# The issue points of indirect row transfers, set by a running count of streamed matmul time

## The chip, the cores and the metric

The kernel runs on one core of a Trainium2 chip. The metric is device time in microseconds (us), the median of three runs. TensorE (PE in the profile) does the matrix products, VectorE (DVE), ScalarE (ACT) and GpSimd (POOL) the elementwise work, SyncE (SP) only issues transfers. Transfers whose rows are scattered by a list of indices ("indirect") are issued by POOL.

## The reference

Two stages follow each other. A long convolution of each of 8 sequences (5056 steps, 128 channels, f32) with one filter, by FFT:

```
Xf = np.fft.rfft(x, n=L, axis=1); Hf = np.fft.rfft(h, n=L, axis=0)     # L = 2 * 5056
y = np.fft.irfft(Xf * Hf[None, :, :], n=L, axis=1)[:, :S, :]
```

Then each of the 40448 resulting rows goes through one of 16 experts, picked by two argmaxes (4 groups, 4 experts in each), and is scaled by the two softmax weights:

```
h = np.maximum(xg[mask_e] @ w1[g, e], 0.0)       # 128 -> 1024
out[tok_idx] = combined[:, None] * (h @ w2[g, e])  # 1024 -> 128
```

## The kernel before

The FFT is a chain of small matmuls in three rounds (`ROUNDS`), of three sequences each; the filter takes one place in round 0. In a round, `stage1` transforms along one axis, `groups` transforms along the other, multiplies by the filter's spectrum and transforms back (`forward`, `product`, `inverse`), and `side` does the last transform, one octave (8 of 64 steps) at a time. `side` of a round runs beside stage 1 and groups of the next round, and that of round 2 beside the experts. An octave gives 10 or 15 tiles of 128 token rows; it computes their gate, and with it the place of each row in a table `srt` in DRAM, sorted by expert. Each tile is then scattered into `srt` by one indirect transfer (`scatter`, line 873; 320 of them). From step 0 of the experts on, blocks of 512 rows of one expert are gathered from `srt` (`ffn_x`, line 1284), multiplied through both layers as split f32r matmuls (`mm1`, lines 1383 to 1385, `mm2`, lines 1401 to 1403; 8 steps for a block), transposed and scaled into a tile `orow` (`out_store`), and scattered into `out` by indirect transfers of 128 rows (`scatter_out`, line 1450). Blocks 2 to 29 send half their rows into a buffer `outd` first, and fetch them back later (`take`), so that these go out with later blocks. 59 blocks are fixed at build; the rest of each expert runs in a tail of conditional blocks (`ffn_tail`).

The order on each engine is that in which the program records its work, and a table `main` of closures sets it, into which `weave` sets the steps of `side`. Rows that wait for their scatter stand in the list `self.sends`, output rows in `self.due`. In the kernel before, transfers are sent at fixed places of the program: one `send` in each `product`, after an `inverse`, after every fourth step of stage 1, after pieces of `side` (`beside`), and one after most expert steps; `scatter_out` at certain steps of a block's plan ("o"). Each transfer that is sent so is made to wait for a matmul by `behind`, by way of `self.mark`, the matmul recorded last at certain lines:

```
    def behind(self, ins):
        if self.mark is not None:
            info = mybir.DependencyInfo(mybir.DependencyClass.Sync, mybir.DependencyReason.DATA)
            self.tc.add_manual_dep(ins.ins, self.mark.ins.name, info, reason="transfers are issued one by one")
```

POOL works in order. So a transfer goes out when its matmul has ended, its data are there, and POOL has issued the one before it. `drain` empties `self.sends` before the expert blocks that read the rows of a round. What waits for a transfer's landing: the reuse of `rw` tiles (ACT, line 798), of `orow` tiles (DVE, line 1421), the gathers from `srt` (SP, line 1284), the fetching back (`take`, SP, line 1444), and the eighth transfer after it on POOL (eight semaphores, DMASW0 to DMASW7, take turns).

## Time and profile before

| | us |
|---|---|
| median of 3 runs | 1722.85 (1707.83, 1722.85, 1723.93) |
| profiled execution | 1721.78 |
| its span, first to last instruction | 1720.1 |
| PE busy in the span | 1627.1 (95%) |
| DVE, ACT, POOL busy | 1311.6, 1084.3, 753.7 |
| mean granted clock of TensorE | 0.987 of full speed |

The rounds' stage 1 and groups fill the span up to about 650 us, round 0 without any indirect transfer; the first stands at 190.5 us. The experts' fixed blocks run from about 656 to 1450 us, the tail from there to the end. A PE that is busy 95% of the time leaves some 93 us in which it waits, and where these lie is what the rows below are for.

### The profile page before, as it was taken

To read this page: it belongs to the slowest core of one execution; us is meant where nothing else is said; L and a number is where in the kernel's file an instruction comes from. 1 tells how busy PE (TensorE), PEld (TensorE's weight loads), DVE (VectorE), ACT (ScalarE), POOL (GpSimd) and SP (SyncE) were. 2 spreads that over 40 slices of the span, in tenths; PEclk is the share of its full clock that TensorE was granted. 3 is DMA by queue.
4 is the path that set the end of the run, shared out by engine and by line. 5 is a ranking of instruction groups with operands and counts; after the bars stand their busy time and mean duration, and the time that the engine had idled before them with its cause. 6 is when DMAs were issued, how large, how long until landed. Compare 5 with 4: busy or idle time off the path is not lost. (4 is left out here: it accounts for less than half of the span.)

```text
span 1720.1 us, 46979 instructions
## 1 busy us (share of the span) xinstructions
PE 1627.1 (95%) x16576; PEld 1259.0 (73%) x16576; DVE 1311.6 (76%) x2917; ACT 1084.3 (63%) x2145; POOL 753.7 (44%) x730
## 2 busy tenths in 40 slices
PE   8998899998899987999999999999999999999997
PEld 7667755557655555777777777787788877888987
DVE  6654588775488778688877778888788888887888
ACT  5564444444445445677777777676677777777775
POOL 1451233342364545145454446145555655334545
PEclk9999999999999999999999999999999999999999
DMA  7797577867678866676666756456955687555667
GB/s 212 240 288 219 168 243 243 260 223 209 180 218 275 256 221 197 165 173 179 179 180 158 175 152 169 113 160 201 194 156 163 169 213 205 140 141 146 160 159 173
DMA packets 403936, 330.20 MB, mean 192 GB/s; under 512 B 167708, under 2 KB 347425, under 8 KB 403672
## 3 DMA queue, kind: packets, MB, share of 16 engines
q1 hardware_dynamic: 374808, 271.01, 58.5%
q0 software_dynamic: 20608, 41.79, 7.4%
q10 hardware_dynamic: 8256, 14.10, 2.9%
q8 instruction: 139, 2.28, 0.6%
q14 instruction: 125, 1.02, 0.2%
HBM read 208.00 MB, written 96.86 MB: 177 GB/s over the span
## 5 line engine op out<-in xcount | busy, mean ns | idle before, releaser
L873 POOL DMA_INDIRECT srt<-rw,pos x320 | 331.8, 1037 | 442.9 <-issue 53.5
L1450 POOL DMA_INDIRECT out<-orow,ids x176 | 184.5, 1048 | 252.4 <-PE ptr L1403 69.0
L553 DVE TENSOR_TENSOR y<-pp,hg 128x768 f32<-128x768 f32 (+1 forms) x108 | 92.4, 855 | 88.7 <-ACT hg L543 32.4
L1450 POOL DMA_INDIRECT out<-orow,sids x92 | 96.1, 1045 | 114.1 <-DVE orow L1421 88.4
L601 PE MATMUL pp<-y,cg 64*64 64x384 f32 (+1 forms) x1504 | 125.8, 449 | 14.6 <-DVE m L553 8.3
L533 PE MATMUL pp<-st,cg 64*64 64x192 f32 (+1 forms) x1588 | 120.8, 408 | 2.3 <-issue 1.1
L445 DVE TENSOR_TENSOR st<-pp,odd 128x320 f32<-128x320 f32 x96 | 46.9, 488 | 86.6 <-ACT odd L444 70.3
L614 ACT COPY zs<-pp 128x768 f32<-128x768 f32 (+1 forms) x106 | 75.7, 714 | 53.2 <-PE pp L601 43.0
L1389 DVE SCALAR_TENSOR_TENSOR h3l<-px,h3h 128x512 fp32r<-128x512 f32 (+1 forms) x111 | 74.3, 669 | 38.3 <-ACT h3h L1388 31.9
L601 PEld LDWEIGHTS pp<-y,cg 64*64 64x64 f32 x1504 | 61.0, 134 | 57.1 <-issue 29.9
L1389 DVE SCALAR_TENSOR_TENSOR h0l<-px,h0h 128x512 fp32r<-128x512 f32 (+1 forms) x109 | 73.3, 672 | 37.5 <-ACT h0h L1388 22.3
L754 ACT COPY yT<-py 128x474 f32<-128x474 f32 (+1 forms) x96 | 44.3, 513 | 88.2 <-PE py L747 86.0
L1388 ACT ACTIVATE h0h<-px 128x512 fp32r<-128x512 f32 (+1 forms) x109 | 64.0, 587 | 55.6 <-PE px L1385 39.1
L733 PEld LDWEIGHTS py<-ig,zm 126*64 126x64 f32 x2048 | 76.6, 139 | 29.7 <-issue 18.0
L733 PE MATMUL py<-ig,zm 126*64 126x79 f32 x2048 | 86.9, 237 | 11.4 <-issue 5.5
L533 PEld LDWEIGHTS pp<-st,cg 64*64 64x64 f32 x1588 | 63.2, 134 | 44.8 <-issue 34.3
L1389 DVE SCALAR_TENSOR_TENSOR h2l<-px,h2h 128x512 fp32r<-128x512 f32 (+1 forms) x112 | 75.1, 671 | 26.5 <-ACT h2h L1388 21.2
L553 DVE TENSOR_TENSOR m<-pp,hg 128x768 f32<-128x768 f32 (+1 forms) x108 | 91.3, 846 | 0.0
L1388 ACT ACTIVATE h3h<-px 128x512 fp32r<-128x512 f32 (+1 forms) x111 | 65.4, 589 | 33.2 <-PE px L1385 14.7
L798 ACT COPY rw<-py 128x1024 uint16<-128x1024 uint16 (+1 forms) x88 | 80.8, 937 | 7.0 <-PE ptr L1402 1.6
L1388 ACT ACTIVATE h1h<-px 128x512 fp32r<-128x512 f32 (+1 forms) x111 | 65.3, 588 | 29.8 <-PE px L1385 13.2
L585 POOL TENSOR_TENSOR y<-y,m 128x512 f32<-128x512 f32 x40 | 50.9, 1276 | 74.5 <-DMA hd<-hg 40.8
(478 smaller groups left out, 5129.1 us busy)
## 6 DMA issues: line engine op xcount, KB each, us to landing
wr<-in_moe_w SPq DMA_DIRECT2D x373, 256.0 KB
zd<-zs SPq DMA_DIRECT2D x66, 384.0 KB
zm<-zd SPq DMA_DIRECT2D x64, 378.0 KB
cg<-in_c_g SPq DMA_DIRECT2D x106, 224.0 KB
zd<-zs SPq DMA_DIRECT2D x39, 256.0 KB
hg<-hd SPq DMA_DIRECT2D x68, 128.0 KB
xt<-in_x ACTq DMA_DIRECT2D x52, 160.0 KB
zm<-zd SPq DMA_DIRECT2D x32, 252.0 KB
```

The costliest lines, as they stand in the source:

```text
L445: nc.vector.tensor_tensor(out=all_st[:, 0:2 * HALF, d], in0=even, in1=odd, op=ALU.add)
L533: last = nc.tensor.matmul(px[c * 64:c * 64 + 64, b, to], lhsT=k, rhs=data[:, of], start=begin, stop=i == len(steps) - 1 or p == 0 and i == ...
L553: nc.vector.tensor_tensor(out=t[:, :, 0:w].rearrange("p t (r u d) -> p t r u d", r=2, u=nu), in0=taken(px, part).unsqueeze(1).broadcast_to ...
L585: (nc.gpsimd if r == 0 else nc.vector).tensor_tensor(out=y[:, :, 0:w], in0=y[:, :, 0:w], in1=m[:, :, 0:w], op=ALU.add)
L601: self.mark = nc.tensor.matmul(pz[c][h:h + 64, 0:w], lhsT=wt[c * 64:c * 64 + 64, k + h:k + h + 64], rhs=y[c * 64:c * 64 + 64, part, 0:w], ...
L614: nc.scalar.copy(out=z[:, 0:n, 0:w], in_=pp[:, 0:n, 0:w])
L733: nc.tensor.matmul(pys[q][c:c + 64, col(n, u)], lhsT=zms[q][:, n % QB, k:k + 64], rhs=self.ig[:, 0:NH], start=n % QB == 0 and u == 0, stop ...
L798: nc.scalar.copy(out=od["rw"][i // 2][:, 4 * i % RH:4 * i % RH + n, 0:2 * D].rearrange("p j (h d) -> p j h d", h=2), in_=pt[:, 0:n * D].bi ...
L873: ins = self.nc.gpsimd.indirect_dma_start(out=self.srt, out_offset=bass.IndirectOffsetOnAxis(ap=k["pos"][0:p, j:j + 1], axis=0), in_=k["rw ...
L1388: nc.scalar.activation(out=hh, in_=p, func=AF.Relu)
L1389: nc.vector.scalar_tensor_tensor(out=hl, in0=p, scalar=0.0, in1=hh.bitcast(F32), op0=ALU.max, op1=ALU.subtract)
L1450: ins = self.nc.gpsimd.indirect_dma_start(out=self.a["out"], out_offset=bass.IndirectOffsetOnAxis(ap=ids, axis=0), in_=o, in_offset=None, ...
```

## The change

Transfers are no longer sent from set places in the program. `worked` is called behind nearly every group of matmuls with the time that the group streams (columns times a constant for f32 or f32r), adds it to a running `self.clock`, and sends one transfer when the clock has passed `self.next`. `issued` then sets `self.next` 1.9 us of streamed time further, or 1.4 (1.6 beside the experts) when more than 4 (8) are waiting, and never less than 1.3 us from now. A row is sent no earlier than 1.4 us of streamed time after it has been put on its list. Of `self.sends` and `self.due` the one that has been ready longest goes first, so that rows to `srt` and rows to `out` go by age. All sends up to the tail wait for the last matmul recorded, `scatter_out` too. `out_store` sends by force what is three blocks old, `rows` what is left of the last octave but one, and `drain` and the start of the tail empty the lists as before. `worked` also stands behind the matmuls of `side` (lines 733 and 808) that left no mark before. The core of the diff:

```diff
@@ -38,6 +38,10 @@
 TB, HB = 384, 256
 NC = (NTOK - NE * (BLK + 128) + BLK - 1) // BLK
 NW_MIN = NC
+PACE = {False: (1.9, 1.4, 4), True: (1.9, 1.6, 8)}
+LEAST = 1.3
+READY, SPREAD = 1.4, 0.0
+COL, COLR = 4 / 2400, 1 / 2400 + 25e-6
 NW_MAX = (NTOK + NE * 127) // BLK
 T0, H0 = 1000, 2000
 GP = 128
@@ -242,7 +246,8 @@
         self.dr = ctx.enter_context(tc.tile_pool(name="dr", bufs=1, space=DRAM))
         self.ctx, self.banks = ctx, ExitStack()
         self.pq = self.banks.enter_context(tc.tile_pool(name="pq", bufs=4, space=PSUM))
-        self.turns, self.beside, self.sends, self.mark = 0, "", [], None
+        self.turns, self.beside, self.sends, self.due = 0, "", [], []
+        self.mark, self.paced, self.clock, self.next = None, True, 0.0, 0.0
 
     def share(self):
 
...
             for i, (to, of, w) in enumerate(steps):
-                if i == 1 and p % 2 == 0:
-                    self.mark = last
                         )
-            if p % 2 == 1:
-                self.mark = last
+                self.worked(last, (to.stop - to.start) * COL)
             if r == 0:
                 ht = hgs[p].rearrange("p t (r d) -> p t r d", d=HD)
                 h = px[:, :, 0:2 * UH].rearrange("p r (t w) -> p t r w", t=2)[:, :, :, 0:HD]
...
                 nc.vector.memset(hgs[p][0:1, 2, :], 0.0)
             y = multiply(px, p, 0, "y", 4)
-            self.send()
...
                             stop=u == nu - 1, tile_position=(k, c),
                         )
+            self.worked(last, nu * QB * NH * COL)
             for q in (n // QB, n // QB + 1):
                 k = QB * q % 8 * c1
                 nc.scalar.copy(out=self.yT[:, k:k + QB * c1], in_=pys.pop(q)[:, 0:QB * c1])
-
-        def beside():
-            if self.beside != "experts":
-                self.send()
 
         def lump(k):
             def f():
...
-                at.append((t + 4.7, both(lm, lambda: rows(0), beside), False))
+                at.append((t + 4.7, both(lm, lambda: rows(0)), False))
-                at.append((t + 12.15, lambda o=o, s=sends: self.sends.extend((8 * r + o, f) for f in s), True))
+                at.append((t + 12.15, lambda o=o, s=sends: self.sends.extend((8 * r + o, f, self.clock + READY + SPREAD * i) for i, f in enumerate(s)), True))
-                at.append((t + 3, both(lm, lambda: rows(0), beside), False))
+                at.append((t + 3, both(lm, lambda: rows(0)), False))
...
@@ -890,10 +890,31 @@
 
         if self.sends:
             self.sends.pop(0)[1]()
+            self.issued()
+
+    def issued(self):
+
+        far, close, many = PACE[self.beside == "experts"]
+        gap = close if len(self.sends) + len(self.due) > many else far
+        self.next = max(min(self.next, self.clock) + gap, self.clock + LEAST)
+
+    def worked(self, ins, us):
+
+        self.mark = ins
+        self.clock += us
+        if not self.paced or self.clock < self.next:
+            return
+        ready = [x[0][2] for x in (self.sends, self.due) if x and x[0][2] <= self.clock]
+        if not ready:
+            return
+        if self.due and self.due[0][2] == min(ready):
+            self.scatter_out(1)
+        else:
+            self.send()
 
     def behind(self, ins):
 
-        if self.mark is not None:
+        if self.paced:
             info = mybir.DependencyInfo(mybir.DependencyClass.Sync, mybir.DependencyReason.DATA)
             self.tc.add_manual_dep(ins.ins, self.mark.ins.name, info, reason="transfers are issued one by one")
 
...
-            nc.tensor.matmul(o, lhsT=wh[:, k:k + 128], rhs=xh, start=True, stop=False)
-            nc.tensor.matmul(o, lhsT=wl[:, k:k + 128], rhs=xh, start=False, stop=False)
-            self.mark = nc.tensor.matmul(o, lhsT=wh[:, k:k + 128], rhs=xl, start=False, stop=True)
+            last = nc.tensor.matmul(o, lhsT=wh[:, k:k + 128], rhs=xh, start=True, stop=False)
+            self.worked(last, n * COLR)
+            last = nc.tensor.matmul(o, lhsT=wl[:, k:k + 128], rhs=xh, start=False, stop=False)
+            self.worked(last, n * COLR)
+            last = nc.tensor.matmul(o, lhsT=wh[:, k:k + 128], rhs=xl, start=False, stop=True)
+            self.worked(last, n * COLR)
         hh, hl = (t[:, 0:G * n] for t in self.hs[i % 4])
         p = p[:, 0:G * n]
         nc.scalar.activation(out=hh, in_=p, func=AF.Relu)
...
+        while j is not None and any(d[3] is not None and d[3] <= j - NROW + 1 for d in self.due):
+            self.scatter_out(1)
         if ids is self.lids:
             rows = fx.tile([128, 4, 1], I32, name="sids", bufs=2)
             nc.vector.tensor_copy(out=rows[:, 0:T], in_=ids[:, 0:T, 0:1])
...
-        self.due += [(rows[:, t, 0:1], o[:, t, :]) for t in range(now)]
+        self.due += [(rows[:, t, 0:1], o[:, t, :], self.clock + READY, j) for t in range(now)]
...
             )
-            if timed:
-                self.behind(ins)
+            self.behind(ins)
             self.no_dep("scatter_out", ins)
-        self.due = self.due[n:]
+            self.due = self.due[1:]
+            self.issued()
 
     def keep_ids(self, j):
         nc = self.nc
...
                         )
                 elif q == "o":
-                    if prev and j < NA - 2 and at in (4, 6):
+                    if j < NW_MIN:
                         self.put()
-                        self.send()
                     elif prev:
-                        self.scatter_out(1 if ns == 8 else 4, j < NW_MIN)
+                        self.scatter_out(1 if ns == 8 else 4)
                 elif q == "c":
                     if j + k < end and (j + k, "x") not in self.kept:
                         self.ffn_join_x(j + k)
...
         self.keep_ids(NW_MIN - 1)
         self.scatter_out(len(self.due))
+        self.paced = False
         nw = nc.values_load(self.nbw, min_val=NW_MIN - NC, max_val=NW_MAX - NC)
         nt = nc.values_load(self.nbt, min_val=0, max_val=NE)
         nh = nc.values_load(self.nbh, min_val=0, max_val=NE)
...
                     for k, f in enumerate(s1[r][1]):
                         add(f, W_S1)
-                        if r > 0 and k % 4 == 1:
-                            add(self.send)
                         if r == 0:
                             add(advance(more))
                         if r == 2 and ("end", 0) in mark:
...
                     add(f, FW[k % 8])
                     if k in (8 * (N0 - 2) - 1, 8 * (NA - 2) - 1):
                         add(self.drain)
-                    elif k < 8 * (NA - 2) and (k < 8 * (N0 - 2) or k % 8 not in (3, 4, 5, 6)):
-                        add(lambda: self.send())
-                    elif k >= 8 * (NA - 2) and k % 8 in (7, 0, 1, 2):
-                        add(lambda: self.scatter_out(1, True))
                     if k % 8 == 6:
                         add(lambda: (self.due.extend(self.taken), self.taken.clear()))
                     m, n = k // 8 - NA, (PUT1 - PUT0) // 2

```

The transfers are the same 644, and the order on PE, ACT and SP stays (a piece of gate work moves by a step). What moves is POOL's order and the matmul that each transfer waits for. On POOL from the last rows of round 1 to the end of round 2's (`srt<-rw` is a tile of rows to the sorted table, `out<-orow` 128 output rows), before:

```order
23 L1450 DMA out<-orow,ids 40448x128
24 L873 DMA srt<-rw,pos 331776x260 x3
25 L1450 DMA out<-orow,ids 40448x128
26 L873 DMA srt<-rw,pos 331776x260 x3
27 L1450 DMA out<-orow,ids 40448x128 x7
28 L873 DMA srt<-rw,pos 331776x260
29 L1450 DMA out<-orow,ids 40448x128
30 L873 DMA srt<-rw,pos 331776x260 x5
31 L1450 DMA out<-orow,ids 40448x128
```

The same place with the change:

```order
22 L873 DMA srt<-rw,pos 331776x260 x133
23 L1479 DMA out<-orow,ids 40448x128 x14
24 L873 DMA srt<-rw,pos 331776x260 x15
25 L1479 DMA out<-orow,ids 40448x128 x6
26 L873 DMA srt<-rw,pos 331776x260 x15
27 L1479 DMA out<-orow,ids 40448x128 x6
28 L873 DMA srt<-rw,pos 331776x260 x15
```

Both kinds were mixed one by one; now an octave's 15 tiles go out in one piece, with the output rows of the blocks between two octaves in front of them.

On POOL at the end of the fixed blocks, before (`take` are rows fetched back; PE_49 is PE's semaphore, so a row with it waits for a matmul of its own):

```order
570 L1450 DMA out<-take,kept_ids 40448x128 [waits DMAHW0_49,DMASW0_49,PE_49]
571 L1450 DMA out<-take,kept_ids 40448x128 [waits DMASW1_49,PE_49]
572 L1450 DMA out<-take,kept_ids 40448x128 [waits DMASW2_49,PE_49]
573 L1450 DMA out<-take,kept_ids 40448x128 [waits DMASW3_49,PE_49]
574 L1450 DMA out<-orow,ids 40448x128 [waits DMASW4_49,DVE_49,PE_49]
```

And with the change:

```order
570 L1479 DMA out<-take,kept_ids 40448x128 [waits DMAHW0_49,DMASW0_49]
571 L1479 DMA out<-take,kept_ids 40448x128 [waits DMASW1_49]
572 L1479 DMA out<-take,kept_ids 40448x128 [waits DMASW2_49]
573 L1479 DMA out<-take,kept_ids 40448x128 [waits DMASW3_49]
574 L1479 DMA out<-orow,ids 40448x128 [waits DMASW4_49,DVE_49]
575 L1479 DMA out<-orow,ids 40448x128 [waits DMASW5_49]
576 L1479 DMA out<-orow,ids 40448x128 [waits DMASW6_49]
577 L1479 DMA out<-orow,ids 40448x128 [waits DMASW7_49]
```

The last eight transfers of the fixed blocks had a matmul each to wait for, and are now what is left on the list when the tail begins.

On POOL at the drain of the rows of rounds 0 and 1, before the first gather that needs them, before:

```order
217 L873 DMA srt<-rw,pos 331776x260 [waits DMASW1_49,PE_49,Activation_49]
218 L1450 DMA out<-orow,ids 40448x128 [waits DMASW2_49,DVE_49,PE_49]
219 L873 DMA srt<-rw,pos 331776x260 [waits DMASW3_49]
220 L873 DMA srt<-rw,pos 331776x260 [waits DMASW4_49,PE_49]
221 L873 DMA srt<-rw,pos 331776x260 [waits DMASW5_49]
```

And with the change:

```order
218 L873 DMA srt<-rw,pos 331776x260 [waits DMASW2_49,PE_49]
219 L873 DMA srt<-rw,pos 331776x260 [waits DMASW3_49,PE_49]
220 L873 DMA srt<-rw,pos 331776x260 [waits DMASW4_49]
221 L873 DMA srt<-rw,pos 331776x260 [waits DMASW5_49,Activation_49]
222 L873 DMA srt<-rw,pos 331776x260 [waits DMASW6_49]
223 L873 DMA srt<-rw,pos 331776x260 [waits DMASW7_49]
224 L1479 DMA out<-orow,ids 40448x128 [waits DMASW0_49,DVE_49,PE_49]
```

Four tiles of rows now leave at the drain without a matmul between them, and the first output rows come behind them.

## Rows read from the trace of the kernel before

**Rows 1.** Page, part 1: busy us (share of the span) and instructions.

```profile
PE 1627.1 (95%) x16576; PEld 1259.0 (73%) x16576; DVE 1311.6 (76%) x2917; ACT 1084.3 (63%) x2145; POOL 753.7 (44%) x730
```

**Rows 2.** Windows by stage: us, busy of PE, PEld, DVE, ACT, POOL; clock, DMA, GB/s.

```profile
60.00:130.00 70.00, 68.94 (x1277) 48.45 (x1270) 40.90 (x65) 42.45 (x128) 40.79 (x32) 1.00 0.92 288
190.00:650.00 460.00, 417.54 (x6754) 272.06 (x6753) 338.86 (x797) 216.83 (x483) 187.12 (x185) 0.98 0.74 229
...
700.00:1080.00 380.00, 375.10 (x2691) 298.79 (x2688) 302.18 (x688) 276.64 (x495) 179.79 (x173) 1.00 0.66 169
1080.00:1450.00 370.00, 361.77 (x1620) 291.29 (x1619) 305.43 (x637) 266.27 (x476) 188.28 (x181) 0.99 0.69 178
```

**Rows 3.** PE's waits, 190 to 650 us: releaser, us in total, times, longest.

```profile
PE pp L427 <- issue: 7.7, 17, 1.3
PE pp L601 <- DVE m L553: 7.5, 10, 2.3
...
PE pp L601 <- issue: 4.4, 5, 1.9
...
PE pp L533 <- issue: 3.1, 13, 0.4
PE py L733 <- issue: 2.8, 6, 1.3
```

**Rows 4.** PE's waits, 700 to 1240 us.

```profile
PE ptr L1401 <- ACT h0h L1388: 4.1, 1, 4.1
PE ptr L1417 <- ACT oT L1406: 2.4, 1, 2.4
```

**Rows 5.** POOL's groups: count, busy us, mean ns, idle us before them, releasers.

```profile
L873 POOL DMA_INDIRECT srt<-rw,pos x320 | 331.8, 1037 | 442.9 <-issue 53.5 <-DVE st L446 49.2 <-PE py L747 44.8
L1450 POOL DMA_INDIRECT out<-orow,ids x176 | 184.5, 1048 | 252.4 <-PE ptr L1403 69.0 <-PE pz L1403 68.9 <-PE px L1385 40.2
L1450 POOL DMA_INDIRECT out<-orow,sids x92 | 96.1, 1045 | 114.1 <-DVE orow L1421 88.4 <-issue 16.4 <-DVE lids L1471 6.3
L1450 POOL DMA_INDIRECT out<-take,kept_ids x56 | 57.9, 1033 | 30.6 <-issue 12.5 <-PE px L1384 4.5 <-PE pz L1403 4.4
```

**Rows 6.** POOL's timeline, 1220 to 1236 us: start, us, instruction, idle before it.

```profile
1220.25 1.21 POOL L1450 DMA_INDIRECT out<-take,kept_ids  x1 [4.22 <-PE px L1384]
...
1229.46 0.98 POOL L1450 DMA_INDIRECT out<-orow,ids  x1 [0.30 <-issue]
1230.74 0.98 POOL L1450 DMA_INDIRECT out<-take,kept_ids  x1 [0.31 <-issue]
1233.73 0.98 POOL L1450 DMA_INDIRECT out<-take,kept_ids  x1 [2.01 <-remote]
```

**Rows 7.** ACT's timeline in the same stretch.

```profile
1226.74 0.60 ACT L1388 ACTIVATE h3h<-px 128x512 fp32r<-128x512 f32 x1 [1.05 <-PE pz L1403]
1233.41 0.60 ACT L1388 ACTIVATE h0h<-aux 128x512 fp32r<-128x512 f32 x1 [6.06 <-remote]
```

**Rows 8.** Windows of three packed stretches of transfers.

```profile
681.00:695.00 14.00, 10.93 (x91) 7.57 (x90) 4.27 (x9) 4.23 (x9) 7.88 (x8) 0.76 0.65 169
1066.00:1078.00 12.00, 9.62 (x44) 7.72 (x43) 7.51 (x12) 6.45 (x12) 7.77 (x8) 0.97 0.67 163
1221.00:1238.00 17.00, 12.93 (x51) 9.84 (x50) 10.22 (x25) 7.80 (x16) 11.40 (x12) 0.90 0.99 233
```

**Rows 9.** SP's timeline: the first gather that needs the drained rows.

```profile
697.93 1.26 SPq L1284 DMA_TRANSPOSE xr<-srt  x1
```

**Rows 10.** POOL's and ACT's timelines: last drained rows, use of that gather, first tail transfer.

```profile
693.47 1.01 POOL L873 DMA_INDIRECT srt<-rw,pos  x1 [3.42 <-PE py L747]
...
718.20 0.77 ACT L1333 COPY x<-xr 128x512 uint16<-128x512 uint16 x1
...
1449.78 0.99 POOL L1450 DMA_INDIRECT out<-orow,sids  x1 [5.80 <-DVE orow L1421]
```

**Rows 11.** Line 873's transfers: ns min/median/max, first and last start.

```profile
L873 POOL DMA_INDIRECT srt<-rw,pos x320: 948/977/2885, 190.5 to 1076.1; - x160
```

More of the change, by code (lines that the diff above doesn't have):

```diff
@@ L426, in mm @@
                         for c in range(2):
-                            self.mark = nc.tensor.matmul(
+                            last = nc.tensor.matmul(
                                 pp[c * 64:c * 64 + 64, b, j * 2 * HALF:(j + 1) * 2 * HALF],
@@ L432, in mm @@
                 else:
-                    self.mark = nc.tensor.matmul(
+                    last = nc.tensor.matmul(
                         whole[:, j * 256:j * 256 + N1], lhsT=views[i][:, j * 128:j * 128 + 128], rhs=self.f,
@@ L436, in mm @@
                     )
+            self.worked(last, 2 * (N1 if not fold else 2 * HALF) * COL)
             if h == 0:
@@ L600, in inverse @@
                     for h in (0, 64):
-                        self.mark = nc.tensor.matmul(
+                        last = nc.tensor.matmul(
                             pz[c][h:h + 64, 0:w], lhsT=wt[c * 64:c * 64 + 64, k + h:k + h + 64],
@@ L605, in inverse @@
                         )
+                self.worked(last, w * COL)
             if self.fourth(r, p):
@@ L681, in step @@
                     inverse(k - 2 + i)
-                    if i == 1 or len(self.sends) > 20:
-                        self.send()
             yield
@@ L732, in mm @@
                     k = c * nu + u * HD
-                    nc.tensor.matmul(
+                    last = nc.tensor.matmul(
                         pys[q][c:c + 64, col(n, u)], lhsT=zms[q][:, n % QB, k:k + 64], rhs=self.ig[:, 0:NH],
@@ L736, in mm @@
                     )
+            self.worked(last, nu * NH * COL)
         def rest(n):
@@ L746, in rest @@
                         both = pys[q][c:c + 64, 0:QB * c1].rearrange("p (i u m) -> p i u m", i=QB, u=nu)[:, :, u]
-                        self.mark = nc.tensor.matmul(
+                        last = nc.tensor.matmul(
                             both, lhsT=zt[k:k + QB * RT, d:d + 64],
@@ L770, in f @@
                 rest(4 * k)
-                beside()
             return f
@@ L794, in rows @@
                 k = (4 * i + j) * GP
-                self.mark = nc.tensor.transpose(
+                last = nc.tensor.transpose(
                     out=pt[:, j * D:(j + 1) * D], in_=self.yT[:, k:k + GP], identity=self.ident
                 )
+            self.worked(last, n * D * COL / 2)
             nc.scalar.copy(
@@ L807, in lm @@
             for c in range(4):
-                nc.tensor.matmul(
+                last = nc.tensor.matmul(
                     pl[32 * c:32 * c + 32, 0:nsl * GP], lhsT=self.wge, rhs=self.yT[:, c * nsl * GP:(c + 1) * nsl * GP],
@@ L811, in lm @@
                 )
+            self.worked(last, nsl * GP * COL)
             od["lT"] = cx.tile([128, 4 * GP], F32, name="lT", bufs=1)
@@ L853, in side @@
                 at.append((t + 2, lump(2 * o + 1), False))
-                at.append((t + 3, both(lm, lambda: rows(0), beside), False))
-                at.append((t + 4, both(lt, lambda: rows(1), beside), False))
-                at.append((t + 5, both(*more, beside), False))
+                at.append((t + 3, both(lm, lambda: rows(0)), False))
+                at.append((t + 4, both(lt, lambda: rows(1)), False))
+                at.append((t + 5, both(*more), False))
                 at += [(t + 4.02 + 3.3 * k / (NMATH + REST2), advance(ops), True) for k in range(NMATH + REST2)]
-                at.append((t + 7.4, lambda o=o, s=sends: self.sends.extend((8 * r + o, f) for f in s), True))
+                at.append((t + 7.4, lambda o=o, s=sends: self.sends.extend((8 * r + o, f, self.clock + READY + SPREAD * i) for i, f in enumerate(s)), True))
         at.sort(key=lambda x: x[0])
@@ L1400, in mm2 @@
             hh, hl = (t[:, (f % G) * n:(f % G) * n + n] for t in self.hs[i % 4])
-            nc.tensor.matmul(p, lhsT=wh[:, k:k + 128], rhs=hh, start=f == 0, stop=False)
-            nc.tensor.matmul(p, lhsT=wl[:, k:k + 128], rhs=hh, start=False, stop=False)
-            self.mark = nc.tensor.matmul(p, lhsT=wh[:, k:k + 128], rhs=hl, start=False, stop=f == 7)
+            last = nc.tensor.matmul(p, lhsT=wh[:, k:k + 128], rhs=hh, start=f == 0, stop=False)
+            self.worked(last, n * COLR)
+            last = nc.tensor.matmul(p, lhsT=wl[:, k:k + 128], rhs=hh, start=False, stop=False)
+            self.worked(last, n * COLR)
+            last = nc.tensor.matmul(p, lhsT=wh[:, k:k + 128], rhs=hl, start=False, stop=f == 7)
+            self.worked(last, n * COLR)
     def out_evac(self, n, c):
@@ L1444, in take, with scatter_out @@
         self.nc.sync.dma_start(out=t, in_=self.outd[2 * i:2 * i + 2].rearrange("b p t d -> p b t d"))
-        self.taken = [(self.kept_ids[:, 4 * i + m:4 * i + m + 1], t[:, m // 2, m % 2]) for m in range(4)]
-    def scatter_out(self, n, timed=False):
-        for ids, o in self.due[:n]:
+        self.taken = [(self.kept_ids[:, 4 * i + m:4 * i + m + 1], t[:, m // 2, m % 2], 0.0, None) for m in range(4)]
+    def scatter_out(self, n):
+        for ids, o, _, _ in list(self.due[:n]):
             ins = self.nc.gpsimd.indirect_dma_start(
@@ L1474, in ffn_early @@
         self.blk, self.kept = {}, {}
-        self.due = []
         self.ffn_x(0)
```

5 lines of the change are left out of this document (2 added, 3 removed).

## The prediction

> **What bounds the kernel now.** I read the page's busy shares first: PE is busy 1627.1 of 1720.1 us [rows 1], so the change can only win in the 93 us in which PE waits, and in time that PE spends at its lower clock. The windows by stage say where the waiting lies [rows 2]. From 190 to 650 us, where the rows of rounds 0 and 1 are scattered beside stage 1 and groups, PE is idle 460 - 417.5 = 42.5 us. From 700 to 1450 us it is idle only 4.9 + 8.2 = 13.1 us, though POOL has as much to do there (180 and 188 us). From 60 to 130 us, in round 0, no row is scattered, the DMA engines are busier (0.92) than anywhere later, and PE is idle 1.1 of 70 us: load on the DMA engines alone doesn't stop it. (Round 0 also lacks the side work, so this doesn't prove that transfers do.)
>
> PE's waits from 190 to 650 us [rows 3] show two kinds. Some end with a named engine, such as DVE's product (7.5 us). Four large ones, 7.7 + 4.4 + 3.1 + 2.8 = 18.0 us, are put down to "issue": nothing that the profile shows held PE. In the experts two single waits stand out, 4.1 and 2.4 us, both for ACT [rows 4].
>
> Then POOL's timeline around the first of these [rows 6]. From 1221.76 us on, transfer follows transfer at 1.28 us, the shortest pitch that POOL has (0.98 busy, 0.30 between): eight up to 1230.74. ACT starts nothing between 1226.74 and 1233.41 us, 6.06 us of it idle [rows 7], and PE stands behind ACT. The window around it has PE's clock at 0.90 of full [rows 8]: clock is 2.4 or 1.2 GHz, so half clock for a fifth of 17 us. The other two packed stretches, around 681 and 1066 us, also hold an idle PE (3.1 and 2.4 us) and a lower clock (0.76 and 0.97). That is the reading on which the forecast rests: **long runs of transfers at 1.28 us go with stops of every engine**; single ones, and pairs, in the experts don't.
>
> **The change, part by part.** There are 644 transfers before and after [rows 5]. Their number, size, POOL's 1.0 us for each, and all other engines' work stay. So the cost is in where they stand.
>
> To see this I took from the built order which matmul each transfer waits for, laid it on the time at which that matmul ended in the trace, and let POOL go no faster than 1.28 us. This is an estimate that leaves PE where it was. Of 551 distances between transfers up to 1450 us, 253 are now 1.45 us or less; with the change 55. Runs of five or more fall from 18 to 3. The median distance goes from 1.61 to 1.93 us. So the change does what it says but in three places: seven in a row near 498 us (a forced send of an old octave), twelve from 695 to 709 us (the drain, and the output rows that waited behind it), and some fourteen from 1441 us on (what the list still holds when the tail begins, and then the tail's own first four, which stand at 1449.78 us now [rows 10]).
>
> 1. Experts, 700 to 1450 us. The two waits beside packed runs go: 4.1 + 2.4 us [rows 4]. Clock: 0.10 of 17 us and 0.03 of 12 us, 1.7 + 0.4 us [rows 8]. **-8.6 us.** The bounds are 0 (the stops come from something else) and -13.1 - 2.1 = -15.2 us (all idle time of the stage goes). I take the value of the two rows, since the other waits there are short and not beside long runs.
>
> 2. Stage 1 and groups, 190 to 650 us. Of 180 distances 62 are close now and 16 will be. If a transfer's closeness is what costs, 46/180 of the 18.0 us marked "issue" go: **-4.6 us**. Bounds: 0, and -18.0. I stay near the small end since the distances here were mostly wide already (median 1.9 us, then 2.2), and the waits on DVE and ACT aren't touched.
>
> 3. The drain. Now the stretch from 681 to 695 us costs 14 - 10.9 = 3.1 us of idle time and 0.24 of 14 us = 3.4 us of clock, 6.4 us, for seven transfers in a row [rows 8]. With the change twelve follow each other some 10 us later. By length that would be 11.0 us, 4.6 more; if one stop is one stop, nothing more; if the stop was chance, 6.4 less. I take **+1.5 us**, near the middle of the first two.
>
> 4. The start of the tail. Fourteen in a row where now ten stand between 1429 and 1443 us with pauses. By the run at 1221 us a stop there costs 4.1 + 1.7 = 5.8 us [rows 4, 8]; bounds 0 and +5.8, I take half, **+2.9 us**.
>
> 5. New waits that I cost at nothing. The last drained row is issued at 693.47 us and SP's gather for block 4 starts at 697.93 [rows 9, 10], having waited for it. The estimate puts that row at 701.1 us, so the gather, and the weights and tiles that SP loads behind it, start some 7.6 us later. The gathered rows are used at 718.20 us [rows 10], 20 us after the gather started, so some 12 us are left; if the landing took more, PE would wait by as much. Reuse of `rw` and `orow` tiles: rows leave up to 12 us later than now, output rows up to 31 us earlier or 15 us later; laid on the times at which ACT and DVE write these tiles, the smallest margin is 3.8 us (an `rw` tile at 218 us). The fetching back by SP keeps over 20 us. POOL's other work between, four memsets in round 2's stage 1, stands behind as many transfers as before. The calls of `worked` cost no instruction.
>
> Sum: -8.6 - 4.6 + 1.5 + 2.9 = -8.8 us. The profiled execution took 1721.8 us, 1.1 less than the median of the three runs; I take its **1713 us** as the forecast. Its own range, from the terms' nearer bounds, is 1705 to 1720. One of the three runs took 1707.83 us with the same program, so what stops the engines differs from run to run by about as much as I expect to win.
>
> **Rivals.**
> A. The distance isn't what costs. For it: only three long runs stopped PE, and most runs of five or six in the experts did not; the stops may come from the loads, gathers and fetches that fall on the same moment (DMA share 0.99 in the window at 1221 us [rows 8]), and then they land somewhere else. Against: the calm window of round 0 at a share of 0.92. Time: 1722 us. Chance 0.25. Of this chance 0.05 is for one mechanism: a transfer is held not by its neighbour but by a DVE operation beside it, wherever it stands. Held transfers would be long issues on POOL; the median of 320 is 977 ns, the shortest 948, the longest 2885 [rows 11], so few are. The Trainium skill states such a rule ("SBUF — State Buffer", section "SBUF: two separate sides"): GpSimd can't write a transfer's descriptors while a VectorE operation holds the port that the two share. By it the sum would be 0 and the time A's, and the row speaks mostly against it.
>
> B. Distance counts more than I take it to. All idle time marked "issue" from 190 to 650 us (18.0), the 13.1 us of the experts and 2.1 us of clock would be 33 us; two thirds of it, since some of it surely has other causes, is 22: 1700 us. For it: this stage holds most of PE's idle time, and one run took 1707.83 us. Against: isolated transfers there still fall beside many short matmuls. Chance 0.30. Beside it stands a rule of the Trainium skill ("Runtime: NRT & Kernel Launch", section "Instruction fetch mechanics"): each sequencer fetches its program ahead in blocks through a DMA queue of its own, and this is mostly hidden. If "issue" were such a fetch held up by transfers, B would gain most; no run here shows it.
>
> C. The packed runs get dearer, and it is slower. The three places hold 7 + 12 + 14 = 33 transfers at the shortest pitch. The stop at 1221 us cost 5.8 us for eight (0.7 each), that at 681 us 6.4 us for seven (0.9 each): 33 times 0.8 is 26, less the 6.4 paid now, +20 us, if nothing is won elsewhere: 1742 us. It decides if every run of seven or more stops the engines. Against: in the tail four at 1.28 us are the rule, and the second and third of the places are where PE has work queued. Chance 0.11.
>
> The forecast has 0.34. A difference under 1%, 17 us, can't be told from none here. Faster by more (under 1705.6 us): 0.28 of B and 0.06 of the forecast's lower end, 0.34. Slower by more (over 1740): 0.09 of C. Within: 0.57. The range 1694 to 1729 us leaves out the lower end of B (0.08) and C (0.11).
>
> **What would show it.** In the profile after: distances of POOL's transfers mostly 1.6 us or more; no wait of PE for ACT over 2 us between 700 and 1440 us and no window with a lowered clock there (step 1); "issue" waits from 190 to 650 us of some 13 us in place of 18 (step 2); idle time and clock around 695 to 710 us as now around 681 to 695 (step 3), and a wait near 1445 us (step 4); the gather of block 4 near 705 us with no wait of ACT for it (step 5). I would be wrong if stops of several us appear in the experts beside well-spaced transfers (A), if PE's idle time in the groups falls by over 10 us (B), or if each packed run shows a stop (C).

## The result, and the profile after

The changed kernel takes **1695.78 us** (median of 6 runs, 1686.83 to 1698.89), the kernel before 1721.31 (median of 6): a ratio of **0.9857 [0.9832, 0.9883]**, 25 us less. The forecast was 1713, the range 1694 to 1729. So direction and range hold, the range by 1.8 us only, and the size is three times what was forecast; the time comes nearest rival B's 1700. On another chip, on which both kernels are faster, the change wins nothing, and on two more chips of that kind none of its variants does (below). That is the larger finding.

The page after, part 1, answers to [rows 1]:

```profile
PE 1603.9 (95%) x16576; PEld 1253.0 (74%) x16576; DVE 1316.5 (78%) x2917; ACT 1086.3 (64%) x2145; POOL 756.5 (45%) x730
```

PE's busy time fell by 23.2 us with the same 16576 matmuls; its idle time in the span only from 93.0 to 89.7. So most of the gain sits inside what the page calls busy: matmuls that take longer from start to start, and time at the lower clock. The windows by stage (busy us of PE, PEld, DVE, ACT, POOL, then clock, DMA share, GB/s) answer to [rows 2]:

```profile
60.00:130.00 70.00, 69.86 (x1296) 49.26 (x1292) 41.54 (x65) 42.55 (x127) 41.52 (x34) 1.00 0.94 293
190.00:650.00 460.00, 416.97 (x6883) 274.60 (x6884) 352.18 (x820) 226.70 (x500) 194.22 (x186) 0.99 0.77 237
...
700.00:1080.00 380.00, 376.23 (x2635) 300.31 (x2634) 310.95 (x732) 278.93 (x499) 180.01 (x174) 1.00 0.64 164
1080.00:1450.00 370.00, 362.13 (x1641) 297.37 (x1640) 309.46 (x614) 273.65 (x484) 185.88 (x181) 0.99 0.70 181
```

From 190 to 650 us PE is idle as long as before (43.0 us, 42.5 before), but 129 more matmuls fit into the window. Equal windows of two kernels hold different work; so I matched the n-th matmul of the one trace with the n-th of the other and cut both at the same matmuls. Idle is time with no matmul recorded, in the tail up to the last matmul; lost to clock is half of the time at 1.2 GHz, whether PE works in it or not.

| stretch (before, us) | length before, after | difference | idle | lost to clock |
|---|---|---|---|---|
| to the first transfers (4 to 181) | 176.5, 180.3 | +3.8 | 7.9, 11.6 | 1.7, 1.7 |
| round 1 (181 to 418) | 237.7, 227.4 | -10.3 | 22.0, 21.4 | 6.8, 0.0 |
| round 2 (418 to 669) | 250.9, 240.9 | -10.0 | 28.5, 23.7 | 5.1, 6.8 |
| around the drain (669 to 711) | 42.2, 42.1 | -0.1 | 3.6, 4.3 | 3.4, 1.7 |
| experts (711 to 1056) | 344.7, 343.2 | -1.5 | 2.5, 2.1 | 0.0, 0.0 |
| experts (1056 to 1441) | 384.8, 369.2 | -15.6 | 9.7, 1.7 | 3.4, 0.0 |
| tail (1441 to the end) | 279.1, 286.4 | +7.3 | 7.7, 13.9 | 2.2, 6.5 |

The distances between transfers are near what the estimate said: up to the tail 75 of 542 are 1.45 us or less (55 by the estimate, 253 of 550 before), runs of five or more fell from 18 to 1, the median rose from 1.61 to 1.85 us. Of the three long runs that the estimate named, only that at the start of the tail is there in full; in rounds 1 and 2, where seven were to stand, no run is over four, and at the drain eight stand between 671.69 and 681.16 us, not twelve. PE's waits from 190 to 650 us (releaser, us, times, longest), against [rows 3]:

```profile
PE pp L603 <- DVE m L556: 7.0, 7, 2.2
PE py L734 <- ACT rw L797: 6.6, 3, 3.6
PE pp L432 <- issue: 5.0, 11, 0.9
...
PE py L734 <- issue: 2.1, 4, 1.3
...
PE pp L603 <- issue: 1.8, 5, 0.6
PE pp L537 <- issue: 1.7, 6, 0.8
```

The four "issue" waits make 10.6 us (18.0 before). In the experts nothing of [rows 4] is left; the largest wait from 700 to 1240 us is

```profile
PE ptr L1429 <- DVE h1l L1413: 0.8, 1, 0.8
```

After that comes a new one, the largest wait from 1240 us to the end:

```profile
PE px L1404 <- issue: 7.3, 1, 7.3
```

It lies at the start of the tail. POOL's timeline there (start, us, instruction, idle before it) is the pattern of [rows 6]: thirteen in a row without a pause, from 1408.62 us to 1424.04.

```profile
1411.19 0.98 POOL L1479 DMA_INDIRECT out<-take,kept_ids  x1 [0.30 <-issue]
...
1416.32 0.98 POOL L1479 DMA_INDIRECT out<-orow,ids  x1 [0.30 <-issue]
...
1424.04 0.98 POOL L1479 DMA_INDIRECT out<-orow,sids  x1 [0.30 <-issue]
```

And ACT's timeline is that of [rows 7], only longer: its last instruction before the stop, its first behind it.

```profile
1412.73 0.77 ACT L1354 COPY x<-xr 128x512 uint16<-128x512 uint16 x1
1422.93 0.60 ACT L1412 ACTIVATE h0h<-px 128x512 fp32r<-128x512 f32 x1 [9.43 <-remote]
```

The windows of the drain and of this stop, against [rows 8]:

```profile
1411.00:1432.00 21.00, 13.13 (x46) 9.76 (x45) 8.34 (x17) 7.18 (x14) 10.77 (x11) 0.76 0.43 115
682.00:696.00 14.00, 12.70 (x69) 9.37 (x67) 6.36 (x11) 7.99 (x14) 5.21 (x6) 0.88 0.94 207
```

In the first, PE is idle 7.87 us, 7.25 of them in one stop from 1417.06 us on, and its clock is at half from 1421.2 to 1431.5 us. That is 0.24 of 21 us, 5.1 us; 1.5 of them fall into the stop itself, so that the two don't add up. PE's next matmul starts at 1424.31 us, beside the last transfer of the run. POOL doesn't stop: it issues at 1.28 us all through it.

### The profile page after: what moved, and what is told of

It reads as the page before. It is cut to its first block, busy times and chain, and to the rows that moved or that the text cites. A ratio compares the mean times of both kernels' runs of the same rounds, so it can differ in the third digit from the quotient of the medians.

```text
span 1693.6 us, 46994 instructions
## 1 busy us (share of the span) xinstructions
PE 1603.9 (95%) x16576; PEld 1253.0 (74%) x16576; DVE 1316.5 (78%) x2917; ACT 1086.3 (64%) x2145; POOL 756.5 (45%) x730
## 5 line engine op out<-in xcount | busy, mean ns | idle before, releaser
L873 POOL DMA_INDIRECT srt<-rw,pos x320 | 336.0, 1050 | 427.1 <-PE py L793 69.8
L603 PE MATMUL pp<-y,cg 64*64 64x384 f32 (+1 forms) x1504 | 121.5, 443 | 11.8 <-DVE m L556 7.0
L1413 DVE SCALAR_TENSOR_TENSOR h0l<-px,h0h 128x512 fp32r<-128x512 f32 (+1 forms) x109 | 73.4, 673 | 38.8 <-ACT h0h L1412 26.5
L734 PEld LDWEIGHTS py<-ig,zm 126*64 126x64 f32 x2048 | 74.1, 137 | 29.0 <-issue 15.6
L734 PE MATMUL py<-ig,zm 126*64 126x79 f32 x2048 | 83.0, 235 | 11.6 <-ACT rw L797 6.6
```

The source lines that it names most:

```text
L603: last = nc.tensor.matmul(pz[c][h:h + 64, 0:w], lhsT=wt[c * 64:c * 64 + 64, k + h:k + h + 64], rhs=y[c * 64:c * 64 + 64, part, 0:w], start ...
L734: last = nc.tensor.matmul(pys[q][c:c + 64, col(n, u)], lhsT=zms[q][:, n % QB, k:k + 64], rhs=self.ig[:, 0:NH], start=n % QB == 0 and u == ...
L873: ins = self.nc.gpsimd.indirect_dma_start(out=self.srt, out_offset=bass.IndirectOffsetOnAxis(ap=k["pos"][0:p, j:j + 1], axis=0), in_=k["rw ...
L1413: nc.vector.scalar_tensor_tensor(out=hl, in0=p, scalar=0.0, in1=hh.bitcast(F32), op0=ALU.max, op1=ALU.subtract)
```

## The experiments

The runs of one set share a chip and the runs of the kernel before on it. The first four fell on a chip on which the kernel before takes 1718.02 us, nearly as in the result (1721.31); the later ones on chips on which it takes 1656 to 1659. I call these chips of the **first** and of the **second kind**. No chip was measured in two sets, so the record doesn't tell a property of the chip from what else ran on it at that time.

### Bursts: the same mean distance, packed

Order by age, counted matmuls and mean distance stay; only each n-th distance is long (n = 2, 4, 8). The short ones are 1.3 us of streamed time, which takes longer on the chip wherever PE waits:

```diff
         gap = close if len(self.sends) + len(self.due) > many else far
+        self.sent = getattr(self, "sent", 0) + 1
+        n = BURST[self.beside == "experts"]
+        gap = n * gap - (n - 1) * LEAST if self.sent % n == 0 else LEAST
```

> The changed kernel, with transfers sent in pairs: 1.3 us of streamed time between the two, then so long that the mean distance stays the same. Order by age, list lengths and the matmuls that are counted stay. Counted in the built order, about 156 of 546 distances up to the tail are 1.45 us or less (55 in the changed kernel, by the same count), but only 3 runs of 7 or more. Long runs cost (theory T): within 6 us of the changed kernel, 1694 to 1702 us, and no stop of all engines beside a pair. Every close distance costs (R2, 26 us for some 200 of them): 100 more are +13 us, 1709. Distances don't matter, the order by age or the matmuls that are waited for do (R1): 1696, within 5.

> The same in fours. About 228 of 546 distances are close, 74 runs of 3 or more, few of 5 or more. T: a little, +3 to +12 us (1699 to 1708), since four take some 4 us, and the stops seen so far stood beside runs of seven or eight. R2: +22 us, 1718. R1: 1696, within 5.

> The same in eights. About 264 of 546 distances are close, and runs of five or more are 22 as in the kernel before (20 by the same count). T: the gain goes, +20 us or more (1716 or over), with PE idle over 2 us and a lowered clock beside several of the runs. R2: +27 us, 1723. R1: 1696, within 5, up to +5 more where a buffer is freed later.

Measured, with the distances counted in each trace up to the tail (in the traces the eights are broken up by waits for data, so that no run is over six; the changed kernel's row is the result's, with its own runs of the kernel before):

| kernel | us | ratio to before | close distances | runs of 5 or more |
|---|---|---|---|---|
| changed | 1695.78 | 0.9857 [0.9832, 0.9883] | 75 of 542 | 1 |
| in twos | 1693.72 | 0.9854 [0.9828, 0.9880] | 133 of 539 | 1 |
| in fours | 1698.61 | 0.9876 [0.9837, 0.9916] | 184 of 539 | 1 |
| in eights | 1706.37 | 0.9914 [0.9885, 0.9942] | 223 of 538 | 14 |
| before | 1718.02 | 1 | 253 of 550 | 18 |

R2 falls: 58 more close distances than in the changed kernel cost nothing, and 109 more nothing clear of the spread. T's figure for the eights, the whole gain, is missed: they keep 12 of the 24 us. And R1 isn't excluded by the time alone, since it allowed the eights up to 1706 us. Where the close distances stand, and what the same matmuls take there, says more (one profiled execution each; the cuts are those of the table above: rounds 1 and 2 are 181 to 669 us of the trace before, the experts 711 to 1441):

| kernel | close in rounds 1 and 2 | us there | close in the experts | us there |
|---|---|---|---|---|
| changed | 22 of 183 | 468 | 44 of 335 | 713 |
| in twos | 20 of 183 | 463 | 102 of 333 | 711 |
| in fours | 25 of 183 | 470 | 149 of 333 | 713 |
| in eights | 25 of 183 | 475 | 186 of 332 | 718 |
| before | 63 of 186 | 488 | 181 of 346 | 730 |

**In the rounds the bursts pack nothing**: distances of 1.3 us of streamed time come out longer there, so the versions have the same few close ones, and their 463 to 475 us show how far executions differ without packing. Of the 16.2 us by which the profiled eights are longer than the profiled twos, 12.7 lie there and can't be put down to close distances. In the experts the packing is real. The changed kernel, twos and fours take 711 to 713 us, the eights 718: packing costs 5 to 7 us there. But with as many close distances as before they keep some 12 of the 17 us that the change won there. Their windows (as those above) show no long stop,

```profile
700.00:1080.00 380.00, 374.20 (x2620) 297.69 (x2619) 308.31 (x718) 276.26 (x496) 180.53 (x174) 1.00 0.65 167
1080.00:1400.00 320.00, 318.32 (x1455) 261.90 (x1454) 272.00 (x556) 238.45 (x425) 154.26 (x153) 1.00 0.68 181
```

with the clock at 1.00 throughout; PE's longest wait from 700 to 1400 us is 1.5 us. So **packing is shown to cost 5 to 7 us in the experts**; in the rounds it wasn't tested.

The traces hold one more sign of it, on an engine that issues none of these transfers. SP's register instructions (MOVE and FUSED_REGOPS) wait for no data; their median is 0.05 us. From 700 to 1400 us the number that took over 0.6 us is 13 before, 0 in the changed kernel, 1 in twos, 9 in fours and 11 in eights. In the kernel before, all 13 started while the third or a later transfer of a close run was being issued, where only 125 of the stage's 770 stand. So runs of close transfers do hold up another engine on this chip, mostly without a stop of PE.

### An empty list at the tail's start

```diff
+        if self.clock > 1000:
+            many = 2
         gap = close if len(self.sends) + len(self.due) > many else far
```

> The changed kernel, but from 1000 us of streamed time on the shorter distance (1.6 us) holds from more than 2 waiting transfers on, not 8, so that the list is nearly empty when the tail begins: some 6 packed transfers there in place of 14. The changed kernel's trace shows PE idle 7.25 us at 1417.06 us and half clock from 1421.2 to 1431.5 us (5.1 us). T: that stop goes, -8 to -12 us (1684 to 1688). R1 and chance (the stop belongs to the branch into the tail, where every engine loads registers): the stop stays, 1696 within 3.

**1681.98 us, 0.9786 [0.9749, 0.9824]**: 11.7 us less than the twos and some 12 less than the changed kernel, by their ratios. T had 8 to 12. With the matmuls matched, 11.4 us of it lie between 1415 and 1440 us of the changed kernel's trace, at the stop. It is the fastest version on a chip of the first kind. POOL's timeline at its tail's start, and the window there:

```profile
1399.83 1.05 POOL L1481 DMA_INDIRECT out<-orow,ids  x1 [0.30 <-issue]
...
1403.74 0.98 POOL L1481 DMA_INDIRECT out<-orow,ids  x1 [0.30 <-issue]
1407.97 0.97 POOL L1481 DMA_INDIRECT out<-orow,sids  x1 [3.25 <-DVE orow L1452]
```

```profile
1396.00:1417.00 21.00, 21.00 (x99) 17.32 (x98) 17.34 (x33) 15.88 (x29) 10.29 (x11) 1.00 0.68 186
```

The branch into the tail, with its register loads, is still there, and PE doesn't wait. Twos, fours and eights, whose lists were not shortened, have 9, 16 and 10 close transfers in a row there, and each has the stop (PE's longest wait from 1385 to 1440 us):

```profile
PE px L1408 <- DVE h0l L1417: 8.3, 1, 8.3
PE px L1408 <- issue: 8.0, 1, 8.0
PE px L1408 <- issue: 7.5, 1, 7.5
```

So the stop belonged to the long run, not to the branch.

### Halves, distance alone, order alone, and what the chip decides

Three more sets were to split the gain. `oldg` sends at the places of the kernel before, and with its marks, up to the experts, `olde` from there on; `order` prefers rows to `srt`; `spaced` keeps the old places and order, but a place only asks:

```diff
+    def place(self, out=False):
+        if not self.old():
+            return
+        if sum(x == out for x in self.asked) < len(self.due if out else self.sends):
+            self.asked.append(out)
...
         if not self.paced or self.clock < self.next:
             return
+        if self.asked:
+            if self.asked.pop(0):
+                self.scatter_out(1)
+            else:
+                self.send()
+        return
```

(`oldg` and `olde` send in `place` at once.) The edit of `order`:

```diff
-        if self.due and self.due[0][2] == min(ready):
+        if not (self.sends and self.sends[0][2] <= self.clock):
```

> Beside stage 1 and groups (up to some 655 us) transfers are sent at the places of the kernel before and wait for its matmuls; beside the experts and at the start of the tail all is as in the changed kernel. Laid side by side by PE's matmuls, the two traces give the change 20 us there (10 in each of rounds 1 and 2). If each stretch keeps what its trace shows (theory S): 1696 + 20 = 1716 us. By the forecast's step 2 (4.6 us): 1700. If stops are chance or move on to later work (rival): within 4 us of 1696. Packing alone (T) allows little here, since four to eight in a row cost 5 to 8 us in these rounds in the runs with bursts: 1702 to 1706.

> The other half: the changed kernel up to the experts, the old places beside the experts; the tail then begins with few waiting transfers, as before. The traces give the change 17 us in the experts and take 12 at the start of the tail. S: 1696 + 17 - 12 = 1701 us, with a wait of several us beside one or two long runs in the experts. The forecast's step 1 alone (8.6 us): 1693. If the 4.1 us wait at 1230 us of before was chance: 1684 to 1690, as the kernel with the short list at the tail's start (1682).

> The kernel before's places, order and kinds, but a place only asks for a transfer; it goes out when 1.6 us of streamed time have passed since the last. By the same count 108 of 551 distances are close (342 by this count in before, 55 in the changed kernel), and few transfers wait at the tail's start. If distance is all that counts (T): 1682 to 1690 us, as the kernel with the short list at the tail's start. If the order by age, or which matmul is waited for, gives the rest, as the burst of eight suggests (it lost only 10 of 26 us): 1700 to 1708.

> The changed kernel, but rows to srt go first whenever one is ready, and output rows after them, whatever their age. Distances and matmuls waited for are the same one by one. If the order by age matters: 1700 us or more, with waits of DVE for an output tile or of ACT for a row tile beside the experts. If it doesn't: 1696, within 3.

> The kernel of the run 'spaced' once more, since that run fell on a chip on which the kernel before itself takes 1656 us and nothing made a difference. On a chip on which the kernel before takes some 1718 us: if distance is all that counts (T), 0.977 to 0.983 of before (the changed kernel with the short list at the tail's start had 0.979); if the order by age, or which matmul is waited for, gives the rest, 0.989 to 0.995. On a chip on which before takes some 1656 us: 1.000, within 0.003.

> The kernel of the run 'oldg' once more. On a chip on which the kernel before takes some 1718 us: if the 20 us that the traces show beside stage 1 and groups belong to the change there (S), 0.997 of before; by the forecast's step 2 (4.6 us) 0.988; by chance or stops that move on, 0.986 within 0.003. On a chip on which before takes some 1656 us: 1.000, within 0.003.

> The kernel of the run 'spaced' a third time, with the changed kernel beside it on the same chip. Where the kernel before takes some 1718 us: if distance is all that counts (T), 0.977 to 0.983 of before, below the changed kernel by the 12 us of its tail's start; if the order by age or the matmuls that are waited for give the rest, 0.989 to 0.995, above the changed kernel. Where before takes some 1656 us: 1.000, within 0.003.

> The changed kernel itself, unchanged. Where the kernel before takes some 1718 us: 0.986 of it, as it did. Where before takes some 1656 us: 1.000 to 1.002, since a version with the same distances and waits ('order') had 1.0008 there; a gain of over 0.5% there would mean that what the change wins doesn't hang on the chip.

Each set fell on another chip, all three of the second kind:

| kernel | us | before, same chip | ratio |
|---|---|---|---|
| `oldg` | 1657.39 | 1656.46 | 1.0015 [0.9992, 1.0038] |
| `olde` | 1655.59 | 1656.46 | 0.9989 [0.9972, 1.0006] |
| `spaced` | 1654.73 | 1656.46 | 0.9997 [0.9976, 1.0018] |
| `order` | 1658.93 | 1656.46 | 1.0008 [0.9989, 1.0027] |
| `spaced`, again | 1658.19 | 1658.56 | 1.0012 [0.9991, 1.0033] |
| `oldg`, again | 1656.87 | 1658.56 | 0.9995 [0.9980, 1.0011] |
| `spaced`, a third time | 1656.96 | 1657.42 | 0.9997 [0.9975, 1.0019] |
| the changed kernel | 1656.40 | 1657.42 | **1.0011 [0.9989, 1.0034]** |

Here nothing that was varied matters: old places or new, close or wide, by age or not. None of these runs separates the theories, since there is nothing to separate. They show something else. `olde` issues beside the experts the same transfers in the same order as the kernel before; POOL's timeline where [rows 6] stood, and PE's window over it:

```profile
1171.81 0.98 POOL L1500 DMA_INDIRECT out<-take,kept_ids  x1 [0.30 <-issue]
...
1178.37 0.98 POOL L1500 DMA_INDIRECT out<-orow,ids  x1 [0.30 <-PE pz L1450]
...
1184.79 0.98 POOL L1500 DMA_INDIRECT out<-take,kept_ids  x1 [0.30 <-DVE w3l L1368]
```

```profile
1168.00:1186.00 18.00, 18.00 (x85) 14.90 (x84) 15.61 (x37) 13.25 (x24) 13.14 (x13) 1.00 1.01 283
```

Eleven in a row, all but one at 1.28 us, DMA share 1.01, and PE is busy 18.00 of 18 us at full clock; on a chip of the first kind the same work cost 4.1 us of idle time at a share of 0.99 [rows 8]. The changed kernel on such a chip, at the start of its tail, where seventeen follow each other closely, the last eleven at 1.28 us without a pause, POOL and PE:

```profile
1382.73 0.97 POOL L1479 DMA_INDIRECT out<-take,kept_ids  x1 [0.30 <-issue]
...
1402.73 0.98 POOL L1479 DMA_INDIRECT out<-orow,sids  x1 [0.30 <-issue]
```

```profile
1381.00:1404.00 23.00, 23.00 (x107) 19.04 (x106) 18.95 (x38) 17.23 (x31) 17.53 (x18) 1.00 0.72 181
```

The same program, and no stop where it had one of 7.25 us. SP's register instructions agree: none takes over 0.6 us in any of the eight traces of this kind, `olde` with 187 close distances in the experts among them. So **a run of transfers at 1.28 us doesn't stop the engines by itself: it can do so on chips of the first kind, and did not on those of the second.**

## Why the forecast was right, and where it was mis-sized

The reading on which it rested held on chips of the kind that it was read from, and at the places in the experts that it named. That the time lies in the range is in part luck: two terms were far too small, and only the stop at the start of the tail, 11.4 us, of which the sum had a quarter, kept the time above 1694. Term by term (measured by the matched stretches):

| step | forecast | measured |
|---|---|---|
| 1, experts | -8.6 | -17.1 |
| 2, stage 1 and groups | -4.6 | -20.3 |
| 3, drain | +1.5 | -0.1 |
| 4, start of the tail | +2.9 | +7.3 |
| stretch without transfers | 0 | +3.8 |

The sum of the right column is -26.4 us; the profiled execution went from 1721.78 to 1695.24, 26.5 less.

**Step 1** was right in kind: both waits of [rows 4] went, and no clock below full is left from 700 to 1400 us. At the two places that it named, the matched traces give 6.1 us (1225 to 1241) and 4.2 us (1069 to 1085), 10.3 in all and near the 8.6; the other 7 lie elsewhere. So the term is half of what was measured. Idle time fell by 8.4 us (6.5 forecast) and clock gave 3.4 (2.1 forecast), but 5.3 us came from a place that the sum left out: matmuls that the profile counts as busy, and which start later after one another. What I called the upper bound, 15.2 us of all idle time and clock, was no bound for that reason.

**Step 2** is the term that was most mis-sized. The "issue" waits fell to 10.6 us, by 7.4 (forecast: to some 13). Of the 20.3 us, idle time makes 5.4 and clock 5.1; the other 9.8 us are again within busy time. Whether the scale, 46 of 180 close distances, was the wrong one isn't shown, since no version with other distances in these rounds ran on a chip of the first kind. And versions that are alike there take 463 to 475 us, so that 20 us is itself known only to some 6 either way. The matching of one program on two chips shows the same form: the changed kernel's matmuls from 403 to 713 us of the result's trace take 22 us longer there than on the last chip of the second kind. From one matmul's start to the next, 38 delays of 0.2 to 1 us make 14.3 us of it (10 of that size go the other way, 3.7 us), four longer ones 5.2, and most are too small to stand out in a list of waits.

**Step 3** was 1.6 us off: 1.3 us idle at 682.3 us and a clock of 0.88, no more than before. But the run there was eight long, not the twelve that it costed, so its scaling by length wasn't tested. **Step 4** was named at the right place, but with half of a stop; it is a whole one, and longer than that at 1230 us (7.25 us idle in place of 4.1). **Step 5** held: the gather of block 4 starts later against PE's work, and nothing waits for it,

```profile
681.10 1.48 SPq L1305 DMA_TRANSPOSE xr<-srt  x1
```

Its clock time is earlier than the 697.93 us of [rows 9], because all before it got shorter. PE's matmul at 697.93 us before is at 674.4 after, so the gather moved by 6.7 us against it; the estimate was 7.6. PE's waits above hold none for it. The +3.8 us in the stretch without transfers is chance: that stretch took 174.6 to 176.8 us in the four traces of the burst and short-list versions on such a chip.

**Rivals.** C's time fell, but its condition hardly came: of its three packed places the first wasn't packed, the second had eight in a row and 1.3 us of idle time, and only the third, the tail's start, had the length that C costed, and a stop. B had the right time by a sum of other parts: its sign, idle time in the groups down by over 10 us, wasn't there (5.4). Its instruction fetches are not the cause of the large stop. In the stretch from 1408 to 1426 us the trace shows packets of two queues alone (packets, MB, share of 16 engines),

```profile
q1 hardware_dynamic: 4518, 1.58, 39.4%
q0 software_dynamic: 470, 0.94, 15.0%
```

while the instruction queues of the page have 139 and 125 packets in the whole run and none here. The Trainium skill ("Runtime: NRT & Kernel Launch", section "Instruction fetch mechanics") calls such fetches mostly hidden; in this stretch none ran, so it shows nothing for or against the page. A was given a quarter. On a chip of the first kind it is wrong as it stood: the shorter list at the tail's start is worth 11.4 us, and packing in the experts costs 5 to 7. On those of the second kind it is right. Its variant, a transfer held by VectorE, isn't seen: line 873's transfers have the same median as in [rows 11],

```profile
L873 POOL DMA_INDIRECT srt<-rw,pos x320: 954/977/2596, 194.9 to 1054.8; - x160
```

and so the rule of the Trainium skill ("SBUF — State Buffer", section "SBUF: two separate sides") plays no visible part in the gain.

**What stays open.** In rounds 1 and 2, where the change won 20 us, no run on a chip of the first kind varied the distances, the places or the order: close distances, the old places and the matmuls waited for there, and the order by age can all hold it. In the experts some 12 of the 17 us are there with packed eights too; 10.3 of the 17 are the two stops beside runs of six and eight, and the eights have runs of five and six without one, so how long a run must be, or what must coincide with it, isn't shown. The run that was to tell (`spaced`) fell three times on a chip where nothing costs. Nor was it shown what makes one chip stop, or whether it is the chip at all and not other work on it at the time. Its DMA engines aren't slower in the steady state: the 5,011 packets of 4096 bytes in POOL's queue take a median of 159 ns in the result's run and in `order` on a chip of the second kind.

## What to carry to other kernels

Measure a change in the placing of transfers on more than one chip before it is kept or dropped: here the same edit is worth 1.4% on chips of one kind and nothing on the other. Where a long run of indirect transfers falls on a busy PE, breaking it up was never slower, and on a chip of the first kind emptying the list before a point where it must be flushed was worth as much as half of the whole edit. When a variant is to test one thing, count in its trace, stage by stage, that it varied it: the bursts packed the experts and not the rounds. When a trace holds stops that nothing in it releases, expect also delays inside the busy time, and size a gain by matching the two kernels' instructions, besides the list of waits.

## What the runs showed of the hardware that was not expected

- The kernel before has medians of 1718 and 1721 us on chips of the first kind and of 1656 to 1659 on three of the second, while runs on one chip lie within 1.2% of each other. The changed kernel differs by 39 us in the same way (1695.78 and 1656.40). Its page on the last chip:

```profile
PE 1582.6 (96%) x16576; PEld 1242.7 (75%) x16576; DVE 1315.8 (80%) x2917; ACT 1088.6 (66%) x2145; POOL 757.5 (46%) x730
```

  DVE, ACT and POOL are busy as long as in the result's run (1316.5, 1086.3, 756.5 us); only PE's busy time (1603.9 there) and the waits differ.
- During the stop at 1417 us a sequencer that waits for no data was slowed too: of SP's eight register instructions from 1412.9 to 1425 us three took 0.68 to 0.71 us, and from 1412.97 to 1419.34 us its instructions start in steps of about 0.70 us. They do so too in the stop of the kernel before, from 1225.24 to 1233.36 us. From 700 to 1400 us 99 of 100 register instructions of the changed kernel take under 0.33, the median 0.05.
- The clock was at 1.2 GHz beside both longer stops: from 1421.2 to 1431.5 us, beginning 4.2 us into the 7.25 us without matmuls, and from 1234.4 to 1237.8 us in the kernel before, behind 4.1 us. By the matched traces the two stops cost 11.4 and 6.1 us, some one and a half times their idle time.
